# Attention and two mixtures on one core: the first group's product with w_out stands one group later, with three smaller edits

## Chip, cores and metric

The kernel runs on one core of a Trainium2 chip. The metric is the device time of one execution in microseconds; three runs of the kernel before had a median of 963.05 us (961.12 to 963.38).

## What is computed

Three layers stand behind one another. The reference, cut to what matters:

```python
scores = where(sink | window, q @ k.T / sqrt(D), -1e9)   # 4 x 8 heads, 768 positions, D = 64
x  = softmax(scores) @ v                                  # 4 sinks, window of 128; x: 3072 x 512
h  = maximum(maximum(x @ w1, x @ w2), x @ w3)             # 512 -> 768
x2 = h @ w_out                                            # 768 -> 512
# routing: the (token, expert) pairs of x2 @ w_gate in falling order, at most 384 tokens per expert
out[mask_e] = relu(x2[mask_e] @ u1[e]) @ u2[e]            # 8 experts, 512 -> 1024 -> 512
```

## The kernel before, in words

**Tokens** come in 8 groups of 384. For each group, four pairs of heads go through attention (`Attn`), then the first mixture (`Moe1.group`, L295 on), then the product with w_out (`Moe1.x2`, L322 on). Products are kept near single precision by splitting each operand into a high and a low part (an ACT copy and a DVE subtraction, L28 and L29) and summing three matmuls.

**Attention** of one pair: scores on PE (L141 to L144), masked into a tile T by DVE (L147 to L155), softmax on ACT (L160 to L163), a product on POOL (L166), transposes on PE (L25 into `pt` and `pp`), DVE masks (L182), the product with v on PE (L189 to L202), and the result in `x0` to `x3`, one tile for each of the four pairs. `group` splits these four into X[0] to X[3] before its matmuls; each X has one buffer, so the split waits for the last matmul of the group before.

**The first mixture** of a group has 6 x 3 sums of 12 matmuls of 384 columns (L308), each into one of the two `mm` banks, taken out by ACT (L310) or DVE (L311); the last of three is split into H[f] in the tile `HL` (L316, L317).

**The product with w_out**: `x2` makes 3 x 2 sums of 18 matmuls of 260 columns (L333) from H, into `mm`. Group 0 can't do this at its place, since w_out isn't loaded yet: it writes its six maxima to HBM (`sp`), and `reload` (L345 on) reads them back through the two-deep tile `hm` (L350, on SP's queue), splits them on ACT (L352) and DVE (L353) into the parts of `HL` that the x2 ahead of it has read, and x2 follows. This stands where `g==back`.

**Order.** The loop over groups emits the attention of group g+1 inside group g (`between`, at sums 0, 1, 3 and 4), for group 2 ahead of group 1 (`order1`, with the six loads of w_out in the middle; `emit` raises its priority by `off=60` instructions). One planner orders each engine's instructions from the order in the code, these priorities and its own costs; tiles of a pool are handed out in the order of the code, so group 3 can't have an `mm` bank before the x2 that stands ahead of it.

**Logits.** Groups 5 to 7 multiply H with w_out @ w_gate (`logits`, L370 on): 12 matmuls (L375) into a bank, an ACT copy (L377), and in `rest`, which the next group calls after its sum (1,0), three transposes into a bank and one DVE reduction (L382).

**Routing and experts.** `Route.phase` finds an expert's threshold in six levels; each level is a count on PE (24 matmuls, L435), a short chain on DVE that ends in a comparison (L430), and the next count. `Moe2.expert` has 8 first products (12 matmuls, L637) and 8 second ones (9 matmuls of 512 columns, L630), 168 matmuls in all. The counts for an expert two further on run between them: `behind` ties the i-th count behind the matmul whose place in the expert's list stands in a tuple.

**The last expert** ends with the second products of f=6 and f=7: rows 0 and 1 for f=6, then for f=7, then row 2 for both. Of each row's sum ACT copies one half (L650) and DVE the other (L651), and POOL scatters the row (L652).

```python
for ts in ((0,1),(2,)): second(F-2,ts); second(F-1,ts)
nc.scalar.activation(o if s.n<7 else o[:,0:256],acc[t] if s.n<7 else acc[t][:,0:256],AF.Copy)
if s.n==7: nc.vector.tensor_copy(o[:,256:512],acc[t][:,256:512])
```

Of the kernel before, what the change touches and what calls it, by code (L numbers as in the profile page):

```python
# [221 lines left out]

class Moe1:
    def __init__(s, tc, words,wgate, consts, wpool, main, conv, mm, pt, pss, ident):
        s.tc=tc; s.nc=tc.nc; s.mm=mm; s.pss=pss; s.main=main; s.conv=conv; s.ident=ident; s.consts=consts
        s.src=words; s.wgate=wgate
        s.W=[[wpool.tile([128,4,768],FR,name=f"w{i}{x}") for x in "hl"] for i in range(3)]
        s.WO=None; s.at=None; s.stage=None; s.HL=None; s.nx=0; s.second=None; s.n=0; s.loads=[]
        s.WG=main.tile([128,6,16],FR,name="wgt")
# [139 lines left out]
            nc.scalar.dma_start(x2d[(t0+t)*128:(t0+t+1)*128,:],o)  # L369
    def logits(s,H,t0,LG):  # L370
        nc=s.nc; main=s.main
        ps=s.mm.tile([128,512],FT,name="mm")
        for f in range(6):
            for b in range(2):
                nc.tensor.matmul(ps[0:16,:384],s.WG[:,f,:],H[f][b],start=(f==0 and b==0),stop=(f==5 and b==1))  # L375
        lt=main.tile([128,520],FT,name="xo",bufs=1)[0:16,:384]
        nc.scalar.activation(lt,ps[0:16,:384],AF.Copy)  # L377
        def rest():
            p=s.mm.tile([128,512],FT,name="mm")
            for t in range(3):  # L380
                flip(nc,p[:,t*16:(t+1)*16],lt[:,t*128:(t+1)*128],s.ident[0:16,0:16])
            nc.vector.tensor_reduce(LG[:,t0:t0+3,:],p[:,0:48].rearrange("p (t b e) -> p t e b",t=3,b=2),axis=AX.X,op=OP.add)  # L382
        return rest
# [183 lines left out]
class Moe2:  # L567
# [53 lines left out]
    def expert(s,X,ev,idx,mid=None):  # L621

        nc=s.nc; F=8; s.n+=1; s.mms=[]
        acc=[s.acc.tile([128,512],FT,name=f"acc{t}") for t in range(3)]
        H=[None]*F; W=[None]*F
        def second(f,ts=range(3)):
            for t in ts:
                n=0
                for a,b in ((0,0),(0,1),(1,0)):
                    s.mms.append(nc.tensor.matmul(acc[t],H[f][a][:,t*128:(t+1)*128],W[f][1][b],start=(f==0 and n==0),stop=(f==F-1 and n==2))); n+=1  # L630
        for f in range(F):
            if f==5 and mid is not None: mid()
            W[f]=s.weights(ev,f)
            ps=s.mm.tile([128,512],FT,name="mm"); n=0
            for k in range(4):
                for a,b in ((0,0),(0,1),(1,0)):
                    s.mms.append(nc.tensor.matmul(ps[:,:384],W[f][0][a][:,k,:],X[k][b],start=(n==0),stop=(n==11))); n+=1  # L637
            h,l=(s.part(x,4+f%2) for x in "hl")
            with s.tc.high_priority():
                nc.scalar.activation(h,ps[:,:384],AF.Relu)  # L640
                nc.vector.scalar_tensor_tensor(l,ps[:,:384],0.0,f32(h),op0=OP.max,op1=OP.subtract)  # L641
            H[f]=(h,l)
            if f and (s.n<7 or f<F-1): second(f-1)
        if s.n<7: second(F-1)
        else:
            for ts in ((0,1),(2,)): second(F-2,ts); second(F-1,ts)
        for t in range(3):
            o=s.act.tile([128,512],FT,name="og",bufs=3)
            with s.tc.high_priority():
                nc.scalar.activation(o if s.n<7 else o[:,0:256],acc[t] if s.n<7 else acc[t][:,0:256],AF.Copy)  # L650
                if s.n==7: nc.vector.tensor_copy(o[:,256:512],acc[t][:,256:512])  # L651
            st=nc.gpsimd.indirect_dma_start(out=s.out,out_offset=bass.IndirectOffsetOnAxis(ap=idx[:,t:t+1],axis=0),in_=o,in_offset=None)  # L652
            for q in s.scat: s.tc.declare_no_dep(st.ins,q.ins,reason="other rows")
            s.scat.append(st)

def attention_mixtures(tc,q,k,v,vs,words,wg,u1,u2,out,off=60,spread=(0,1,3,4),native=8,order='a0 a0 a0 a0 w a1 w a1 w a1 w a1 w w a2',order1='a2 o o o o o o a2 a2',back=1,at=(1,0),s1=300,s2=400,nring=6):
    nc=tc.nc
    PS=bass.MemoryType.PSUM
    with ExitStack() as ctx:
# [4 lines left out]
        mm=P("mm",2,space=PS); pst=P("pst",1,space=PS)  # L664
# [71 lines left out]
        def behind(gs,mms,places):  # L736

            for ins,at in zip(gs,places):
                for i in ins:
                    tc.add_manual_dep(i.ins,mms[at].ins.name,mybir.DependencyInfo(mybir.DependencyClass.NoSync,mybir.DependencyReason.DATA),reason="order on TensorE")  # L740
# [22 lines left out]
        for n in range(8):  # L763
            r.groups=[]
            if n<6:
                with tc.high_priority(offset=s2): S.append(step(n+2)); fet(n+2)
            gs,r.groups=r.groups,[]
            E.expert(*G[n],mid=(lambda: trn(n+1)) if n<7 else None)
            if n<6: behind(gs,E.mms,(40,71,92,105,118,131,144,156,165,167) if n==0 else (20,75,85,95,106,117,131,145,156,160) if n==1 else (20,69,79,91,104,117,131,145,156,160) if n<5 else (4,16))


_INS = ['q', 'k', 'v', 'vs', 'words', 'wg', 'u1', 'u2']
# [50 lines left out]
```

## Time and profile before

| | |
|---|---|
| median of three runs | 963.05 us (961.12 to 963.38) |
| the profiled execution's own time | 959.1 us |
| its span, first to last instruction | 957.3 us |
| TensorE (PE) busy | 926.2 us, 97% |
| VectorE (DVE), ScalarE (ACT), GpSimd (POOL) busy | 702.3, 486.5, 256.3 us |
| mean granted TensorE clock | 0.993 |

Matmuls are pipelined: one of 384 columns has a record of about 0.34 us, while the next one starts about 0.17 us behind it. So a stop of PE shows as idle time only as far as it is longer than the tail of the last record; the starts tell it whole. Where the text speaks of a stop, it is the time from start to start less the usual one. The 1.8 us between span and time lie outside the instructions.

### The profile page before, as it was taken

Reading aid. Unit: us, or ns where it says so; the run is one execution under the profiler, and the core shown is the slowest. Engines: PE = TensorE matmul, PEld = TensorE weight load, DVE = VectorE, ACT = ScalarE, POOL = GpSimd, SP = SyncE. Lnnn points to the kernel's source line nnn. Section 1 sums busy time; section 2 is a strip of 40 time slices with the busy share of each in tenths; the row PEclk is TensorE's granted clock in tenths of the full one; section 3 lists DMA queues with packets and bytes.
Section 4 is the critical chain, followed back from the end, with each engine's and each line's share of the span. In section 5 each row is a group of like instructions: output and inputs, shape, how many; then the busy total and the mean of one; then the engine's idle time right before and its main releaser. Section 6 shows DMA issues by size and latency. Waiting matters only on the chain.

```text
span 957.3 us, 18496 instructions
## 1 busy us (share of the span) xinstructions
PE 926.2 (97%) x6552; PEld 849.3 (89%) x6552; DVE 702.3 (73%) x1870; ACT 486.5 (51%) x1329; POOL 256.3 (27%) x271
## 2 busy tenths in 40 slices
PE   6999999989999999999999999999999999999996
PEld 4688899979999999999999998888888888888895
DVE  7876786787887886678885435888999989873321
ACT  5466664776767685576773211433334434344431
POOL 5676536131321221221221000011203122053331
PEclk8999999999999999999999999999999999999999
DMA  8454322332122221122210002634445353564420
GB/s 234 141 196 154 113 79 79 98 116 74 54 69 70 59 82 42 53 80 92 66 57 1 1 1 89 222 115 133 132 135 177 115 163 116 160 188 163 130 70 33
DMA packets 54443, 99.35 MB, mean 104 GB/s; under 512 B 7792, under 2 KB 24688, under 8 KB 54352
## 3 DMA queue, kind: packets, MB, share of 16 engines
q1 hardware_dynamic: 44464, 75.90, 26.3%
q0 software_dynamic: 3840, 12.45, 3.8%
q10 hardware_dynamic: 6048, 9.83, 2.7%
q8 instruction: 51, 0.84, 0.4%
q14 instruction: 40, 0.33, 0.1%
HBM read 82.17 MB, written 16.12 MB: 103 GB/s over the span
## 4 chain that ended last, share of the span: by engine, by line
PE 80%; DVE 7%; issue 5%; ACT 4%; DMA 2%; POOL 1%; SPq 0%; POOLq 0%; DVEq 0%; ACTq 0%
PE mm L308 28%; PE mm L637 12%; PE acc L630 12%; PE mm L333 8%; PE po L201 3%; PE rc L435 3%; PE po L191 2%; PE ps L141 2%; PE pt L25 2%; PE pp L25 2%; PE ps L143 1%; PE ps L144 1%; ACT T_w L162 1%; PE acc L365 1%; PE po L202 1%
## 5 line engine op out<-in xcount | busy, mean ns | idle before, releaser
L630 PE MATMUL acc<-wbh,HL 128*128 128x512 f32 x384 | 132.2, 400 | 0.0
L311 DVE TENSOR_TENSOR hm<-mm,hm 128x384 f32<-128x384 f32 x96 | 53.1, 553 | 50.2 <-PE mm L308 49.1
L333 PE MATMUL mm<-woh,HL 128*128 128x260 f32 (+1 forms) x432 | 87.0, 291 | 2.5 <-ACT xo L335 1.2
L630 PEld LDWEIGHTS acc<-wbh,HL 128*128 128x128 f32 x384 | 71.4, 188 | 12.9 <-ACT HL L640 0.4
L581 ACT ACTIVATE wah<-sa 128x512 fp32r<-128x512 f32 x64 | 40.4, 631 | 83.3 <-PE mm L637 65.6
L581 ACT ACTIVATE wbh<-sb 128x512 fp32r<-128x512 f32 x64 | 40.4, 631 | 72.9 <-PE acc L630 67.3
L630 PE MATMUL acc<-wbl,HL 128*128 128x512 f32 x192 | 76.9, 401 | 0.0
L652 POOL DMA_INDIRECT out_dram<-og,idx x24 | 29.3, 1222 | 170.6 <-ACT og L650 141.0
L333 PEld LDWEIGHTS mm<-woh,HL 128*128 128x128 f32 x432 | 69.3, 191 | 4.5 <-ACT xo L335 1.9
L637 PE MATMUL mm<-HL,wah 128*128 128x384 f32 x256 | 67.6, 341 | 0.0
L308 PE MATMUL mm<-xh,w1h 128*128 128x384 f32 x192 | 66.0, 344 | 0.8 <-ACT hm L310 0.5
L308 PE MATMUL mm<-xh,w0h 128*128 128x384 f32 x192 | 66.6, 347 | 0.0
L308 PE MATMUL mm<-xh,w2h 128*128 128x384 f32 x192 | 66.2, 345 | 0.2 <-ACT hm L310 0.2
L308 PE MATMUL mm<-xl,w0h 128*128 128x384 f32 x192 | 65.4, 341 | 0.0
L641 DVE SCALAR_TENSOR_TENSOR HL<-mm,HL 128x384 fp32r<-128x384 f32 x64 | 35.4, 554 | 40.6 <-ACT HL L640 38.5
L308 PE MATMUL mm<-xh,w1l 128*128 128x384 f32 x192 | 65.2, 340 | 0.0
L308 PE MATMUL mm<-xh,w0l 128*128 128x384 f32 x192 | 64.9, 338 | 0.0
L308 PE MATMUL mm<-xl,w2h 128*128 128x384 f32 x192 | 64.8, 338 | 0.0
L308 PE MATMUL mm<-xl,w1h 128*128 128x384 f32 x192 | 64.8, 337 | 0.0
L308 PE MATMUL mm<-xh,w2l 128*128 128x384 f32 x192 | 64.6, 337 | 0.0
L582 DVE TENSOR_TENSOR wbl<-sb,wbh 128x512 fp32r<-128x512 f32 x64 | 44.0, 688 | 25.0 <-ACT wbh L581 23.6
L333 PE MATMUL mm<-wol,HL 128*128 128x260 f32 (+1 forms) x216 | 61.9, 288 | 0.0
(335 smaller groups left out, 2781.9 us busy)
## 6 DMA issues: line engine op xcount, KB each, us to landing
sa<-in_u_dram SPq DMA_DIRECT2D x64, 256.0 KB
sb<-in_u_dram SPq DMA_DIRECT2D x64, 256.0 KB
HL<-in_words_dram SPq DMA_DIRECT2D x18, 512.0 KB
qn<-in_q_dram SPq DMA_DIRECT2D x88, 96.0 KB
x2d<-xo ACTq DMA_DIRECT2D x15, 256.0 KB
kn<-in_k_dram SPq DMA_DIRECT2D x12, 264.0 KB
st<-in_words_dram SPq DMA_DIRECT2D x6, 512.0 KB
vn<-in_v_dram SPq DMA_DIRECT2D x12, 256.0 KB
```

The lines of the kernel that those rows point to most:

```text
L25: nc.tensor.transpose(out,x,f32(ident))
L201: nc.tensor.matmul(po[:,q:q+n],u['VS'][:,blk,128*h:128*h+128],part[:,c:c+n],start=(part is H and j==0),stop=False,skip_group_check=True)
L308: nc.tensor.matmul(ps[:,:384],s.W[i][a][:,p,f*128:(f+1)*128],X[p][b],start=(n==0),stop=(n==11)); n+=1
L311: else: nc.vector.tensor_tensor(m,ps[:,:384],m,op=OP.max)
L333: mms.append(nc.tensor.matmul(ps[:,:n],H[f][a][:,t*128:(t+1)*128],s.WO[b][:,f,u,c],start=(k==0),stop=(k==17))); k+=1
L435: s.put([s.nc.tensor.matmul(pc[0:s.M,0:k],s.OHR[:,c],TH[:,c,0:k],start=(c==0),stop=(c==23)) for c in range(*r)])
L581: nc.scalar.activation(h,src,AF.Copy)
L582: (nc.gpsimd if s.n>=6 and nm=="wa" else nc.vector).tensor_tensor(l,src,f32(h),op=OP.subtract)
L630: s.mms.append(nc.tensor.matmul(acc[t],H[f][a][:,t*128:(t+1)*128],W[f][1][b],start=(f==0 and n==0),stop=(f==F-1 and n==2))); n+=1
L637: s.mms.append(nc.tensor.matmul(ps[:,:384],W[f][0][a][:,k,:],X[k][b],start=(n==0),stop=(n==11))); n+=1
L641: nc.vector.scalar_tensor_tensor(l,ps[:,:384],0.0,f32(h),op0=OP.max,op1=OP.subtract)
L652: st=nc.gpsimd.indirect_dma_start(out=s.out,out_offset=bass.IndirectOffsetOnAxis(ap=idx[:,t:t+1],axis=0),in_=o,in_offset=None)
```

## The change

`back` goes from 1 to 2: group 0's reload and x2 stand behind group 2's x2 and ahead of group 3. The logits of t0=18 (group 6) and their `rest` take the bank of the pool `pst` (tile `pt`), which attention used for the sinks' transposes, in place of two `mm` banks. In the last expert each row's sum is finished (f=6, then f=7) before the next row's, and ACT copies all 512 columns. For expert 1 the second to sixth count are tied behind matmuls 74, 86, 97, 108, 119 (75, 85, 95, 106, 117 before), for experts 2 to 4 the third and fourth behind 81 and 92 (79 and 91 before).

```diff
--- before.py
+++ after.py
@@ -222,7 +222,7 @@
 
 class Moe1:
     def __init__(s, tc, words,wgate, consts, wpool, main, conv, mm, pt, pss, ident):
-        s.tc=tc; s.nc=tc.nc; s.mm=mm; s.pss=pss; s.main=main; s.conv=conv; s.ident=ident; s.consts=consts
+        s.tc=tc; s.nc=tc.nc; s.mm=mm; s.pss=pss; s.pt=pt; s.main=main; s.conv=conv; s.ident=ident; s.consts=consts
         s.src=words; s.wgate=wgate
         s.W=[[wpool.tile([128,4,768],FR,name=f"w{i}{x}") for x in "hl"] for i in range(3)]
         s.WO=None; s.at=None; s.stage=None; s.HL=None; s.nx=0; s.second=None; s.n=0; s.loads=[]
@@ -369,14 +369,15 @@
             nc.scalar.dma_start(x2d[(t0+t)*128:(t0+t+1)*128,:],o)
     def logits(s,H,t0,LG):
         nc=s.nc; main=s.main
-        ps=s.mm.tile([128,512],FT,name="mm")
+        bank=(lambda: s.pt.tile([128,512],FT,name="pt")) if t0==18 else (lambda: s.mm.tile([128,512],FT,name="mm"))
+        ps=bank()
         for f in range(6):
             for b in range(2):
                 nc.tensor.matmul(ps[0:16,:384],s.WG[:,f,:],H[f][b],start=(f==0 and b==0),stop=(f==5 and b==1))
         lt=main.tile([128,520],FT,name="xo",bufs=1)[0:16,:384]
         nc.scalar.activation(lt,ps[0:16,:384],AF.Copy)
         def rest():
-            p=s.mm.tile([128,512],FT,name="mm")
+            p=bank()
             for t in range(3):
                 flip(nc,p[:,t*16:(t+1)*16],lt[:,t*128:(t+1)*128],s.ident[0:16,0:16])
             nc.vector.tensor_reduce(LG[:,t0:t0+3,:],p[:,0:48].rearrange("p (t b e) -> p t e b",t=3,b=2),axis=AX.X,op=OP.add)
@@ -643,17 +644,16 @@
             if f and (s.n<7 or f<F-1): second(f-1)
         if s.n<7: second(F-1)
         else:
-            for ts in ((0,1),(2,)): second(F-2,ts); second(F-1,ts)
+            for t in range(3): second(F-2,(t,)); second(F-1,(t,))
         for t in range(3):
             o=s.act.tile([128,512],FT,name="og",bufs=3)
             with s.tc.high_priority():
-                nc.scalar.activation(o if s.n<7 else o[:,0:256],acc[t] if s.n<7 else acc[t][:,0:256],AF.Copy)
-                if s.n==7: nc.vector.tensor_copy(o[:,256:512],acc[t][:,256:512])
+                nc.scalar.activation(o,acc[t],AF.Copy)
             st=nc.gpsimd.indirect_dma_start(out=s.out,out_offset=bass.IndirectOffsetOnAxis(ap=idx[:,t:t+1],axis=0),in_=o,in_offset=None)
             for q in s.scat: s.tc.declare_no_dep(st.ins,q.ins,reason="other rows")
             s.scat.append(st)
 
-def attention_mixtures(tc,q,k,v,vs,words,wg,u1,u2,out,off=60,spread=(0,1,3,4),native=8,order='a0 a0 a0 a0 w a1 w a1 w a1 w a1 w w a2',order1='a2 o o o o o o a2 a2',back=1,at=(1,0),s1=300,s2=400,nring=6):
+def attention_mixtures(tc,q,k,v,vs,words,wg,u1,u2,out,off=60,spread=(0,1,3,4),native=8,order='a0 a0 a0 a0 w a1 w a1 w a1 w a1 w w a2',order1='a2 o o o o o o a2 a2',back=2,at=(1,0),s1=300,s2=400,nring=6):
     nc=tc.nc
     PS=bass.MemoryType.PSUM
     with ExitStack() as ctx:
@@ -766,7 +766,7 @@
                 with tc.high_priority(offset=s2): S.append(step(n+2)); fet(n+2)
             gs,r.groups=r.groups,[]
             E.expert(*G[n],mid=(lambda: trn(n+1)) if n<7 else None)
-            if n<6: behind(gs,E.mms,(40,71,92,105,118,131,144,156,165,167) if n==0 else (20,75,85,95,106,117,131,145,156,160) if n==1 else (20,69,79,91,104,117,131,145,156,160) if n<5 else (4,16))
+            if n<6: behind(gs,E.mms,(40,71,92,105,118,131,144,156,165,167) if n==0 else (20,74,86,97,108,119,131,145,156,160) if n==1 else (20,69,81,92,104,117,131,145,156,160) if n<5 else (4,16))
 
 
 _INS = ['q', 'k', 'v', 'vs', 'words', 'wg', 'u1', 'u2']
```

## Rows read from the trace of the kernel before

**Rows 1.** The page's head and its section 1: span, and PE's busy time.

```profile
span 957.3 us, 18496 instructions
...
PE 926.2 (97%) x6552; PEld 849.3 (89%) x6552; DVE 702.3 (73%) x1870; ACT 486.5 (51%) x1329; POOL 256.3 (27%) x271
```

**Rows 2.** Windows: length, busy us (instructions) of PE, PEld, DVE, ACT, POOL; clock; DMA.

```profile
187.00:207.00 20.00, 16.99 (x106) 13.18 (x105) 17.89 (x36) 16.17 (x55) 8.48 (x8) 0.98 0.44 138
207.00:219.00 12.00, 12.00 (x92) 12.00 (x92) 9.00 (x17) 9.36 (x35) 1.51 (x1) 0.89 0.32 96
219.00:274.00 55.00, 55.00 (x366) 54.69 (x365) 45.40 (x94) 38.68 (x117) 15.49 (x20) 1.00 0.21 59
274.00:292.00 18.00, 18.00 (x153) 17.97 (x152) 13.79 (x28) 13.03 (x42) 2.96 (x4) 1.00 0.27 84
```

**Rows 3.** The same windows for the matmuls of line L333 (x2) alone.

```profile
187.00:207.00 20.00, 6.45 (x36) 4.88 (x36) 0.98 0.44 138
207.00:219.00 12.00, 10.06 (x72) 9.78 (x72) 0.89 0.32 96
```

**Rows 4.** The chain that ended last: start, us, what (two x2 sums without a stop).

```profile
214.47 4.39 PE mm L333 x36
```

**Rows 5.** PE's timeline, 194 to 210 us: start, us, instruction [idle before, releaser].

```profile
196.78 0.90 PE L333 MATMUL mm<-woh,HL 128*128 128x260 f32 x2 [0.80 <-DVE HL L353]
...
205.97 0.39 PE L143 MATMUL ps<-kh_w,qs 128*128 128x260 f32 x1 [1.43 <-DVE T_x L153]
```

**Rows 6.** ACT's timeline, 196 to 205 us: a split of the reload.

```profile
196.72 0.52 ACT L352 ACTIVATE HL<-hm 128x384 fp32r<-128x384 f32 x1 [0.80 <-DMA hm<-sp]
```

**Rows 7.** DVE's timeline, 202 to 208 us: the last split of the reload, and X[3]'s.

```profile
202.40 0.56 DVE L353 TENSOR_TENSOR HL<-hm,HL 128x384 fp32r<-128x384 f32 x1
...
206.90 0.55 DVE L29 TENSOR_TENSOR xl<-x,xh 128x384 fp32r<-128x384 f32 x1
```

**Rows 8.** PE's timeline around the logits of t0=18 and their rest.

```profile
540.62 0.34 PE L375 MATMUL mm<-HL,wgt 128*16 128x384 f32 x1
541.43 0.44 PE L308 MATMUL mm<-xh,w1h 128*128 128x384 f32 x1 [0.46 <-ACT hm L310]
...
547.98 0.35 PE L25 MATMUL mm<-ident,xo 16*128 16x16 f32 x3
548.64 0.45 PE L308 MATMUL mm<-xh,w1h 128*128 128x384 f32 x1 [0.30 <-DVE LG L382]
```

**Rows 9.** PE's timeline in expert 3: the third and fourth count.

```profile
780.42 0.51 PE L637 MATMUL mm<-HL,wah 128*128 128x384 f32 x2
781.27 0.77 PE L435 MATMUL rc<-th,ohr 128*128 128x32 bf16 x24 [0.34 <-DVE th L430]
...
784.36 0.52 PE L435 MATMUL rc<-th,ohr 128*128 128x32 bf16 x14
```

**Rows 10.** DVE's timeline in expert 3: the comparison ahead of the fourth count.

```profile
783.13 0.56 DVE L430 TENSOR_TENSOR th<-z,thr 128x768 bf16<-128x768 bf16 x1
```

**Rows 11.** PE's waits, 680 to 860 us: total, times, longest (the only row).

```profile
PE rc L435 <- DVE th L430: 1.5, 4, 0.6
```

**Rows 12.** ACT's timeline at the end: the last two of three half copies.

```profile
948.59 0.38 ACT L650 ACTIVATE og<-acc 128x256 f32<-128x256 f32 x1 [0.32 <-PE acc L630]
949.99 0.38 ACT L650 ACTIVATE og<-acc 128x256 f32<-128x256 f32 x1 [1.02 <-PE acc L630]
```

**Rows 13.** DVE's timeline at the end: the last low part of H, the last half copy.

```profile
946.32 0.56 DVE L641 SCALAR_TENSOR_TENSOR HL<-mm,HL 128x384 fp32r<-128x384 f32 x1 [3.62 <-ACT HL L640]
...
950.40 0.42 DVE L651 COPY og<-acc 128x256 f32<-128x256 f32 x1 [0.97 <-ACT og L650]
```

**Rows 14.** POOL's timeline at the end: first and last of three scatters.

```profile
949.01 0.99 POOL L652 DMA_INDIRECT out_dram<-og,idx  x1 [26.49 <-DVE og L651]
...
951.57 0.96 POOL L652 DMA_INDIRECT out_dram<-og,idx  x1 [0.31 <-issue]
```

**Rows 15.** Groups by line and shape: the whole copies of the other experts (busy us, mean ns).

```profile
L650 ACT ACTIVATE og<-acc 128x512 f32<-128x512 f32 x21 | 12.6, 598 | 2.6 <-PE acc L630 1.3
```

## The prediction

> **What bounds the kernel now.** I read the page's head first: PE is busy for 926.2 of 957.3 us [rows 1], so only stops of PE can be won back, and they have to be found one by one. I read PE's timeline from start to start and found four places that the change touches. The windows come next. In 187 to 219 us, between group 1's x2 and group 2's first matmul, PE is idle for 3.0 us and its granted clock is 0.98 and then 0.89 of full, while DVE is busy for 17.89 of 20 us; in the 73 us behind it PE never stops and the clock is 1.00 [rows 2]. Group 0's x2 stands in that poor stretch [rows 3].
>
> How much is lost there: 36 matmuls of x2 need 4.39 us when nothing stops them [rows 4], so the 108 of one x2 need 13.2. The other records, attention, are PE's busy time less that of x2: 16.99 - 6.45 = 10.5 and 12.00 - 10.06 = 1.9 us [rows 2, 3]. 32.0 - 13.2 - 12.5 leaves **6.3 us lost**: 3.0 idle, 1.3 + 0.4 by the clock (0.11 of 12 us, 0.02 of 20), the rest hidden under the tails of records. What ended the stops is told by PE's timeline: a split of the reload, and DVE being late with attention [rows 5].
>
> **1. The x2 of group 0 moves (`back`).** Its 108 matmuls, 6 + 3 copies on ACT, 12 splits (6 on ACT, 6 on DVE), 6 loads on SP's queue and 3 stores on ACT's all stay; they leave the stretch at 187 us and come between group 2's x2 and group 3. PE's 13.2 us are neither won nor lost. What changes is who covers whom.
>
> At the old place they cover a late X[3]. Group 2 needs it for the last 3 of each sum's 12 matmuls, and its split ends in 207.45 [rows 7], 20 us behind the end of group 1's x2. With x2 gone PE has until then only attention and, in the two `mm` banks, the 9 matmuls of each sum that go without X[3]: 18, which start 0.17 us apart (a record of two is 0.51 long, of one 0.34 [rows 8, 9]), or 3.1 us. But X[3] should come sooner: the reload's six DVE splits of 0.56 and six ACT splits of 0.52 us [rows 6, 7] leave the queues that its chain runs through, 6.4 us together. Bounds: not sooner at all (207.45), and by all of it (201.0). I take 5 us, 202.4, since most of them stand in front of one of the chain's steps. PE then has 9 us of attention (10.5 less what stands behind 202.4) and 3.1 us of group 2 in 15.4 us: 3.3 lost. By the bounds it is 1.9, or 6.9 (20.45 - 10.5 - 3.1) and another 1.3 by the clock.
>
> At the new place the reload is a chain again: each split waits for the x2 ahead of it to have read that part of `HL`, loads 3 to 6 for `hm`, two at a time, and SP's queue issues them among the loads of attention; ACT waited 0.80 us for one of them [rows 6]. While it runs, no matmul of group 3 can fill in (the `mm` banks are handed out in order), only attention of group 4. No trace shows this; the nearest rows are the old place's. Its stops that the reload itself ended come to 1.4 us (0.80 idle, 0.16 under the tail, and the pair of 196.78 that takes 0.90 where 0.40 is usual) [rows 5]; bounds: 0.3, as group 2's x2 loses now next to no time [rows 2], and 6.3, if all the loss goes along. I take 1.4. DVE is free enough: 45.40 of 55 us in group 2 [rows 2]. **Sum of this part: -6.3 + 3.3 + 1.4 = -1.6 us**, by the bounds from -4.1 to +8.2.
>
> **2. The logits' bank.** Now the logits of t0=18 hold one of the two `mm` banks until the last H is split, so group 7's second sum waits for the first one's copy: from 540.62 to 541.43 are 0.81 us where 0.17 is usual, 0.64 lost. In `rest` the next sum waits for DVE's reduction: 547.98 to 548.64 are 0.66 where three transposes need 0.19 (0.35 less a tail of 0.16), 0.47 lost [rows 8]. In the bank of attention's transposes, idle by then (group 7's attention lies behind), neither wait exists; ACT's copy and DVE's reduction stay and nobody waits for them. **-1.1 us**; bounds 0 (another wait falls due there) and -1.3.
>
> **3. The counts' places.** In expert 3 the third count would follow the matmul pair of 780.42 in 780.77 and starts in 781.27, when DVE's comparison ends: 0.50 lost [rows 9]. There are four such stops in experts 1 to 4 [rows 11]. Two more matmuls ahead of it (0.35 us) leave 0.15 in experts 2 to 4: -1.05. The fourth count then follows one matmul sooner (0.23), and its comparison has ended in 783.69, 0.67 before the count [rows 9, 10]: no new wait. In expert 1 the second count moves up by one matmul and the third back by one: about 0.2 of its stop. **-1.2 us**; bounds 0 and -2.1 (1.5 idle [rows 11] and four tails of 0.16).
>
> **4. The last expert.** The sums now end with 6, 12 and 18 matmuls instead of 9, 12 and 18. Row 1's copy starts in 948.59, row 2's in 949.99, so a matmul is 0.233 us, and row 0 would be ready in 947.19 instead of 947.89 [rows 12]. Only three matmuls of f=6 instead of six now cover H[7]: its low part is ready in 946.88 [rows 13], and row 0's sixth matmul wants it some 0.4 us ahead of 947.19, so a stop of 0.15 which all three rows inherit. The copy: now ACT's half and DVE's follow each other (949.99 + 0.38, then 950.40 + 0.42): 0.83 us; the whole one takes 0.60 [rows 12, 13, 15]. POOL issues three scatters 1.28 us apart from 949.01, so the third, in 951.57, waits for POOL and not for its row [rows 14]. Then: row 0's scatter 947.34 + 0.60 + 0.29 = 948.23 (0.29 as before, 947.89 + 0.83 to 949.01), the third no sooner than 950.79 by POOL, and by its row 949.99 + 0.15 + 0.60 + 0.29 = 951.03. **-0.5 us**; bounds -0.8 and +0.15. The Trainium skill speaks against this edit (Perfetto Trace Analysis, Optimizing Scalar/DVE Operations: where ACT or DVE only hold others up, breaking up instructions may let the work end sooner). By that rule halves would run side by side and end 0.42 after the sum, and the whole copy would cost 0.18 us; the rows show one behind the other, so I go by them.
>
> **The sum**: -1.6 - 1.1 - 1.2 - 0.5 = -4.4 us, from 959.1 us of the profiled execution to 954.7. That execution lies 4.0 us below the median of the runs; I carry the difference over: 963.05 - 4.4 = **958.6 us**.
>
> **Rivals.** A measurement of this kernel can tell about 0.3%, 2.9 us, from no change.
>
> *Slower: PE stands still for X[3].* DVE's queue is full there (17.89 of 20 us [rows 2]); if attention of group 3 moves into the time that the reload leaves, X[3] comes no sooner than 207.45. Then 6.9 us are lost at the head of group 2 and 1.3 by the clock, and if the whole old loss comes back behind group 2's x2 too, the part costs 8.2 instead of giving 1.6: 963.05 + 8.2 - 2.8 = 968.5 us. The point from which the kernel is slower at all is X[3] in about 206.8 (12.1 of work and 7.7 of loss behind 187). For it: one wait in one place would be long, and behind the stops of rows 5 the clock of 207 to 219 is 0.89. The Trainium skill (TensorE: Matmul & The Clock Gate, HAM oscillation) says that a waiting PE is throttled and starts the next work at half clock; the trace agrees with its 0.89, and a single long wait would be worse by it than many short ones. Against it: the chain of X[3] runs through ACT and DVE next to the very splits that go. Chance 0.15.
>
> *No change: the loss goes along.* Late attention and a reload in sequence lose as much at the one place as at the other (part 1 is 0), and the planner, which orders anew, gives half of parts 2 and 3 back elsewhere: -1.6, 961.4 us. That includes the case that counts or logits end up where they were. Chance 0.25.
>
> *All is won.* X[3] comes in 201, and group 2's x2 with the reload behind it has attention enough: part 1 at -4.1 and part 3 at -2.1, -7.8: 955.2 us. Chance 0.12.
>
> **The numbers.** My forecast has 0.48. Faster by over 0.3% (below 960.2): 0.48 + 0.12 = 0.60; within 0.25; slower (above 965.9) 0.15. The range from 953.0 to 966.0 takes in the two milder rivals and half of the way to the slower one, and leaves about 0.06 below it and 0.13 above. The forecast's own range is 955 to 961.
>
> **What the profile of the changed kernel would show.** Right: no L333 between some 187 and group 2's first L308, which starts before 206 us; clock near 1.00 in that stretch; L352 and L353 near 265 to 290; no stop in front of group 7's second sum; third counts with stops near 0.15 us; the third scatter 0.5 us sooner before the end. Wrong: a wait of PE L308 for an L29 of over 5 us, a clock below 0.9 near 200, or waits of L333 for L353 and for attention's DVE work of over 4 us behind group 2.

## The result, and the profile after

The changed kernel takes **975.66 us** (median of 5 runs, 975.08 to 976.56) where the kernel before took 961.42 beside it: a ratio of 1.0144, 95% interval 1.0127 to 1.0162. It is 14 us slower. The forecast was 958.6, from the 963.05 of the first three runs, with a range of 953.0 to 966.0; it was wrong in sign and size.

The page's head of the changed kernel, against [rows 1]:

```profile
span 974.4 us, 18527 instructions
...
PE 933.8 (96%) x6552; PEld 852.4 (87%) x6552; DVE 709.8 (73%) x1867; ACT 488.1 (50%) x1329; POOL 259.2 (27%) x271
```

PE issues the same 6552 matmuls. Its busy time is 7.6 us more (tails of records and a slower clock), and the other 9.5 of 17.1 us are idle. To see where, cut the span at the groups' first and last matmuls of L308. The windows of the kernel before (us, busy us of PE, PEld, DVE, ACT, POOL, clock, DMA): group 1's x2 and group 0's; group 2; group 2's x2; group 3; group 3's x2.

```profile
167.10:219.40 52.30, 49.29 (x352) 44.77 (x350) 40.54 (x87) 39.67 (x143) 11.50 (x10) 0.97 0.35 106
219.40:273.40 54.00, 54.00 (x358) 53.71 (x357) 44.63 (x92) 37.68 (x115) 15.49 (x20) 1.00 0.21 57
273.40:292.00 18.60, 18.60 (x157) 18.57 (x156) 14.39 (x29) 13.62 (x43) 2.96 (x4) 1.00 0.30 89
292.00:342.00 50.00, 50.00 (x321) 49.72 (x320) 42.37 (x76) 33.85 (x104) 10.27 (x12) 1.00 0.22 62
342.00:361.80 19.80, 18.77 (x157) 18.48 (x155) 17.06 (x33) 15.08 (x49) 5.42 (x6) 1.00 0.31 94
```

The same five stages of the changed kernel; group 0's x2 is now in the third:

```profile
168.00:187.60 19.60, 19.60 (x152) 18.90 (x151) 13.41 (x35) 13.60 (x52) 1.51 (x1) 1.00 0.22 67
187.60:263.10 75.50, 70.34 (x436) 63.66 (x435) 69.12 (x127) 55.26 (x184) 21.52 (x24) 1.00 0.26 75
263.10:319.40 56.30, 49.16 (x363) 46.72 (x362) 52.14 (x97) 46.61 (x150) 16.41 (x18) 0.94 0.36 110
319.40:364.70 45.30, 45.30 (x284) 45.10 (x283) 32.73 (x65) 26.72 (x88) 7.48 (x8) 1.00 0.16 49
364.70:382.40 17.70, 16.07 (x134) 15.86 (x133) 7.09 (x12) 7.50 (x19) 2.58 (x3) 1.00 0.14 47
```

Idle time alone hides stops under tails, so for each stage I added up, over PE's timeline, how much each matmul started later than is usual behind the one before it ("lost", good to about 1 us a row):

| stage | length before | after | lost before | after |
|---|---|---|---|---|
| to group 2's first L308 | 52.2 | 19.6 | 7.6 | 0.3 |
| group 2 | 54.0 | 75.5 | 1.8 | 12.1 |
| to group 3's first L308 | 18.7 | 56.4 | 0.4 | 14.0 |
| group 3 | 50.0 | 45.3 | 0.9 | 0.7 |
| to group 4's first L308 | 19.7 | 17.7 | 1.8 | 2.4 |
| group 4 to the end of group 7 | 216.9 | 211.6 | 10.4 | 7.9 |
| sum | 411.5 | 426.1 | 22.9 | 37.4 |

The whole difference of the runs (14 us) stands in the last row: +14.5. It comes in two places. **Old place** (first two rows): 9.4 lost becomes 12.4, though the product and its reload are gone. Group 2 ends 11.2 us sooner against the start of group 1's x2 (95.1 instead of 106.3 us), and 13.2 us of work have left. DVE is busy there for 13.41 + 69.12 of 95.1 us, and of the 5.2 us that PE stands idle in group 2 it waits 4.1 for DVE, never longer than 1.0 at a time (the two longest of PE's waits there: in total, times, longest):

```profile
PE ps L143 <- DVE T_x L153: 1.6, 2, 1.0
PE mm L308 <- DVE hm L311: 1.4, 2, 0.8
```

X[3] comes little sooner than before, [rows 7]:

```profile
206.17 0.55 DVE L29 TENSOR_TENSOR xl<-x,xh 128x384 fp32r<-128x384 f32 x1
```

That is 18.6 us behind the end of group 1's x2, where it was 19.9. **New place** (third row): 0.4 lost becomes 14.0, at a granted clock of 0.94. Some 9 us of it stand in 284 to 306 us, where the clock is 0.84, a mean of its two levels (2.4 and 1.2 GHz):

```profile
284.00:306.00 22.00, 17.35 (x105) 15.67 (x105) 21.43 (x39) 18.37 (x61) 5.85 (x7) 0.84 0.44 131
```

Behind a stop of 1.84 us, the one of 291.66 below, matmuls of 260 columns start 0.22 us apart where 0.12 is usual [rows 4], which is the lower level:

```profile
293.80 0.42 PE L333 MATMUL mm<-woh,HL 128*128 128x260 f32 x1
294.02 0.42 PE L333 MATMUL mm<-wol,HL 128*128 128x260 f32 x1
```

As an estimate, the clock took at most 0.16 of 22 us, 3.5 us, of the 14.0; the rest is stops. PE's timeline there, 264 to 303 us, the matmuls before which PE stood idle longest (the bracket: for how long, and for whom):

```profile
267.52 0.39 PE L333 MATMUL mm<-woh,HL 128*128 128x260 f32 x1 [1.17 <-DVE hm L311]
...
273.78 0.39 PE L143 MATMUL ps<-kh_x,qs 128*128 128x260 f32 x1 [1.32 <-DVE T_w L153]
...
288.03 0.51 PE L333 MATMUL mm<-woh,HL 128*128 128x260 f32 x2 [0.46 <-DVE HL L353]
...
291.66 0.56 PE L201 MATMUL po<-H,vsp 128*128 128x256 f32 x3 [1.84 <-DVE x L204]
...
300.35 0.55 PE L25 MATMUL pt<-ident,T_w 128*128 128x128 f32 x3 [0.85 <-POOL T_w L166]
...
302.19 0.56 PE L333 MATMUL mm<-woh,HL 128*128 128x260 f32 x2 [0.96 <-DVE HL L353]
```

Over the stretch PE stands idle for 1.9 us until a split of the reload is done (L352, L353), for 3.9 until attention is (L153, L204, L166), and for 1.2 until group 2's own maximum is (L311). The reload's loads on SP's queue are issued in pairs, since `hm` is two deep:

```profile
261.36 8.52 SPq L350 DMA_DIRECT2D hm<-sp  x2
...
288.00 1.62 SPq L350 DMA_DIRECT2D hm<-sp  x2
...
294.26 0.80 SPq L350 DMA_DIRECT2D hm<-sp  x2
```

and the second and third pair's first copies on ACT start 3.3 and 3.5 us behind them. ACT was busy with attention up to either copy, so a part of this is its own queue; where it did stand and wait for a load, in the kernel before, the copy came 2.4 us behind the issue (194.34 to 196.72 [rows 6]):

```profile
291.27 0.51 ACT L352 ACTIVATE HL<-hm 128x384 fp32r<-128x384 f32 x1
...
297.78 0.53 ACT L352 ACTIVATE HL<-hm 128x384 fp32r<-128x384 f32 x1
```

Last, DVE's timeline shows where the lead of attention ends. In the changed kernel the last half of group 4's attention and the first of group 5's (L204):

```profile
325.98 0.56 DVE L204 TENSOR_TENSOR x<-po,x 64x384 f32<-64x384 f32 x1
...
365.87 0.55 DVE L204 TENSOR_TENSOR x<-po,x 64x384 f32<-64x384 f32 x1
```

and the same two in the kernel before:

```profile
329.89 0.56 DVE L204 TENSOR_TENSOR x<-po,x 64x384 f32<-64x384 f32 x1
...
345.49 0.54 DVE L204 TENSOR_TENSOR x<-po,x 64x384 f32<-64x384 f32 x1
```

Group 4's attention ends at about the same time in both. Then the next write has to wait until `x0` has been split into X[0], which has one buffer, and that is when group 3's matmuls end: 364.7 instead of 342.0. The gap is 39.9 us instead of 15.6. At group 4's first matmul the changed kernel is 20 us behind (382.4 against 361.8). No run gave X a second buffer, so that this is what limits the lead rests on these rows.

**The small edits.** The logits of t0=18 go through the transposes' bank; of two stops of 0.64 and 0.47 [rows 8] there is one left, of 0.28 (559.41 - 558.95 less the usual 0.18):

```profile
558.95 0.33 PE L376 MATMUL pt<-HL,wgt 128*16 128x384 f32 x1
559.41 0.44 PE L308 MATMUL mm<-xh,w2h 128*128 128x384 f32 x1
```

The counts still stop PE four times (PE's waits, 690 to 880 us, against [rows 11]); by the starts, the third counts of experts 2 to 4 now stop for 0.15 us, as reckoned, but the second ones for 0.46:

```profile
PE rc L436 <- DVE th L431: 1.4, 4, 0.5
```

At the end, the last low part of H on DVE, and first and last of the whole copies on ACT and of the scatters on POOL, against [rows 12 to 14]:

```profile
963.93 0.56 DVE L642 SCALAR_TENSOR_TENSOR HL<-mm,HL 128x384 fp32r<-128x384 f32 x1 [3.65 <-ACT HL L641]
```

```profile
965.19 0.60 ACT L651 ACTIVATE og<-acc 128x512 f32<-128x512 f32 x1 [1.29 <-PE acc L631]
...
967.75 0.60 ACT L651 ACTIVATE og<-acc 128x512 f32<-128x512 f32 x1 [0.80 <-PE acc L631]
```

```profile
966.07 0.99 POOL L652 DMA_INDIRECT out_dram<-og,idx  x1 [25.93 <-ACT og L651]
...
968.63 0.96 POOL L652 DMA_INDIRECT out_dram<-og,idx  x1 [0.30 <-ACT og L651]
```

From the low part to the third scatter it is 4.70 us, where it was 951.57 - 946.32 = 5.25: 0.55 won. Every profiled execution with this edit has 4.69 or 4.70, and both without it have 5.25.

### The profile page after: what moved, and what is told of

Its sections match the earlier page's. It is cut to its first block, busy times and chain, and to the rows that moved or that the text cites. A ratio compares the mean times of both kernels' runs of the same rounds, so it can differ in the third digit from the quotient of the medians.

```text
span 974.4 us, 18527 instructions
## 1 busy us (share of the span) xinstructions
PE 933.8 (96%) x6552; PEld 852.4 (87%) x6552; DVE 709.8 (73%) x1867; ACT 488.1 (50%) x1329; POOL 259.2 (27%) x271
## 4 chain that ended last, share of the span: by engine, by line
PE 80%; DVE 9%; issue 5%; ACT 3%; DMA 2%; POOL 0%; SPq 0%; POOLq 0%; DVEq 0%; ACTq 0%
PE mm L308 27%; PE mm L638 12%; PE acc L631 12%; PE mm L333 8%; PE po L201 3%; PE rc L436 3%; PE po L191 2%; PE ps L141 2%; PE pt L25 2%; PE pp L25 2%; PE ps L143 1%; PE ps L144 1%; DVE m L159 1%; PE acc L365 1%; DVE L L197 1%
## 5 line engine op out<-in xcount | busy, mean ns | idle before, releaser
L311 DVE TENSOR_TENSOR hm<-mm,hm 128x384 f32<-128x384 f32 x96 | 53.2, 554 | 60.1 <-PE mm L308 56.1
L333 PE MATMUL mm<-woh,HL 128*128 128x260 f32 (+1 forms) x432 | 85.5, 289 | 3.1 <-DVE HL L353 1.7
L333 PEld LDWEIGHTS mm<-woh,HL 128*128 128x128 f32 x432 | 69.3, 191 | 5.1 <-DVE HL L353 2.4
L308 PE MATMUL mm<-xh,w0h 128*128 128x384 f32 x192 | 66.8, 348 | 1.3 <-ACT xh L28 0.7
L308 PE MATMUL mm<-xh,w2h 128*128 128x384 f32 x192 | 66.6, 347 | 0.8 <-ACT hm L310 0.7
L308 PE MATMUL mm<-xh,w1h 128*128 128x384 f32 x192 | 66.3, 345 | 0.8 <-DVE hm L311 0.8
L308 PE MATMUL mm<-xl,w0h 128*128 128x384 f32 x192 | 65.6, 341 | 0.0
L308 PE MATMUL mm<-xh,w1l 128*128 128x384 f32 x192 | 65.3, 340 | 0.0
L308 PE MATMUL mm<-xl,w2h 128*128 128x384 f32 x192 | 65.0, 339 | 0.0
L308 PE MATMUL mm<-xh,w0l 128*128 128x384 f32 x192 | 64.9, 338 | 0.0
L308 PE MATMUL mm<-xl,w1h 128*128 128x384 f32 x192 | 64.8, 337 | 0.0
L308 PE MATMUL mm<-xh,w2l 128*128 128x384 f32 x192 | 64.8, 337 | 0.0
L166 POOL TENSOR_TENSOR T_w<-T_w,l 128x792 f32<-128x792 f32 x21 | 32.1, 1529 | 114.1 <-DVE l L165 114.1
```

Of the source, the lines that this page charges most:

```text
L166: s.ev['s',u['n']]=nc.gpsimd.tensor_tensor(T,T,l[:,:,None].to_broadcast([128,6,132]),op=OP.mult)
L308: nc.tensor.matmul(ps[:,:384],s.W[i][a][:,p,f*128:(f+1)*128],X[p][b],start=(n==0),stop=(n==11)); n+=1
L311: else: nc.vector.tensor_tensor(m,ps[:,:384],m,op=OP.max)
L333: mms.append(nc.tensor.matmul(ps[:,:n],H[f][a][:,t*128:(t+1)*128],s.WO[b][:,f,u,c],start=(k==0),stop=(k==17))); k+=1
```

## The experiments

All ratios are to the kernel before, run beside each on the same chip; the intervals are of 95%. "Lost" is told as in the table above, from one profiled execution of each.

### Is it the move, or one of the small edits?

The changed kernel with the product at its old place:

```diff
-...,back=2,at=(1,0),...
+...,back=1,at=(1,0),...
```

> The changed kernel with group 0's x2 put back behind group 1's (back=1); the logits' bank, the counts' places and the last expert stay changed. If the move of x2 is the cause of the 14 us (both theories below), this stands at or a little under the kernel before: 959 to 961 us, by what the changed kernel's trace shows of the three small edits (0.55 at the end, 0.4 to 0.8 at the logits, nothing at the counts, whose stops only went from one count to the one ahead of it). If one of the small edits is the cause (theory S), it stands near 970 us or above.

And the kernel before with the move alone:

```diff
-...,back=1,at=(1,0),...
+...,back=2,at=(1,0),...
```

> The kernel before with back=2 alone. If the move is the cause: 976 to 978 us, what the changed kernel takes and the 1 to 1.5 us that the small edits gave. Theory S: 961 us.

Measured: 958.05 us, ratio 0.9987 (0.9973 to 1.0000), and 975.81, ratio 1.0166 (1.0133 to 1.0199). In the first the stages lose what they lost before (7.5, 1.8 and 0.4 in the first three), in the second what they lose after (11.8 in group 2, 13.9 behind it). **The move alone makes the kernel slower**, and the small edits have no part in it.

### What does the reload cost at either place?

The product of group 0 reads the H that is there (group 2's, or group 1's at the old place), so the 6 loads and 12 splits of the reload are left out and 384 rows of group 0 get another group's values:

```diff
-                    M.x2(M.reload(sp),0,LG,x2d)
+                    M.x2(H,0,LG,x2d)
```

At the new place:

> The changed kernel, in which x2 of group 0 multiplies the H of group 2 again: the six loads and twelve splits of the reload are left out (the 384 rows of group 0 get group 2's values), its 108 matmuls stay. Theory R (the reload's chain of loads and splits, with no matmul of group 3 to fill in, makes the 13.8 us that PE loses between 264 and 319 us): about 10 us come back, 964 to 967 us. Theory D (DVE is late with attention from 187 us on, since x2 no longer stands there as work for PE that needs no DVE; PE waits for DVE wherever it stands): only the reload's own DVE time comes back, 3.4 us of splits and perhaps some half clock: 970 to 973 us.

At the old one (with `back=1`):

> back=1 with the small edits, and x2 of group 0 takes group 1's H again: the reload's six loads and twelve splits are left out (the 384 rows of group 0 get group 1's values). It measures what the reload costs at the old place. If it costs there what it costs at the new one (12 us): 946 to 949 us. If the old place hides it but for the 1.4 us of stops that the prediction counted there: 956 to 957 us.

| ratio | product behind group 1 | behind group 2 |
|---|---|---|
| with the reload | 0.9987 (0.9973 to 1.0000) | 1.0144 (1.0127 to 1.0162) |
| without it | 0.9967 (0.9955 to 0.9980) | 1.0054 (1.0039 to 1.0070) |

Down the columns: the reload costs 0.0020, some 2 us, at the old place and 0.0090, some 9 us, at the new one. Along the rows: the move costs 0.0087, some 8 us, even when nothing has to be reloaded, and 15 with the reload. So **about half of the loss is the product's own place, and about half the reload at that place** (each difference is good to some 2 us). Without the reload the stretch behind group 2 loses 3.8 us instead of 14.0 (windows of the kernel without it, group 2 and the stretch behind it):

```profile
188.10:263.50 75.40, 70.25 (x436) 63.57 (x434) 69.06 (x127) 55.10 (x184) 21.54 (x24) 1.00 0.25 73
263.50:301.60 38.10, 35.58 (x294) 34.96 (x293) 28.53 (x55) 25.88 (x84) 9.08 (x10) 1.00 0.25 82
```

### Is PE's time at the old place free?

The changed kernel with group 1's product done twice, which puts 108 matmuls (13.2 us) of nothing where group 0's product stood:

```diff
-                elif g: M.x2(H,3*g,LG,x2d)
+                elif g:
+                    M.x2(H,3*g,LG,x2d)
+                    if g==1: M.x2(H,3*g,LG,x2d)
```

> The changed kernel with group 1's x2 done twice in a row: 108 matmuls, 13 us of PE work that asks for almost nothing of DVE, stand again where group 0's x2 stood before, and nothing else changes. Theory D: PE had no work there that DVE could feed, so the added 13 us cost 0 to 4 us: 976 to 980 us. Theory R, or PE simply being the bound there: they cost 10 to 13 us, 986 to 989 us.

Measured: 976.54 us, ratio 1.0180 (1.0145 to 1.0216), 0.0036 above the changed kernel: 3.5 us for 13.2 us of work (good to some 4 us). The windows from group 1's end to group 2's first matmul, and of group 2:

```profile
168.10:209.50 41.40, 41.40 (x310) 38.02 (x310) 22.48 (x50) 22.91 (x80) 7.01 (x8) 1.00 0.22 69
209.50:262.90 53.40, 53.40 (x353) 53.28 (x352) 45.15 (x91) 39.70 (x128) 12.44 (x14) 1.00 0.23 70
```

Group 2 ends in 262.9, and without the filler in 263.1. PE has no idle time at all: most of the filler stands where PE stopped before. Not all of it, though. The changed kernel has 152 + 436 matmuls in these two windows, so the filler should make 696, and there are 663: 33 matmuls of attention, 3.9 us of PE's work, now follow behind group 2's end, about what the kernel is longer by. So some 9 of the 13 us were free. Nor is the end near 263 one limit: with the filler PE is busy throughout and DVE for 67.6 of 94.8 us, without it DVE for 82.5 of 95.1 and PE waits for it. The kernel without the reload at the old place shows the same as the filler:

```profile
168.20:209.60 41.40, 41.40 (x310) 38.01 (x309) 22.50 (x50) 22.84 (x80) 7.02 (x8) 1.00 0.22 69
209.60:263.00 53.40, 53.40 (x352) 53.28 (x351) 45.18 (x91) 39.68 (x128) 12.39 (x14) 1.00 0.22 65
```

So the 11.2 us by which the changed kernel's group 2 ends sooner are owed to the reload's leaving; the product's leaving gave no sooner end, only those 33 matmuls of attention ahead of it. And even of that lead little lasts: the kernel without the reload is 11.5 us ahead at group 2's end of the one with it at the same place, and 0.0020, 2 us, in the end. Nearly half of the lead is work put off (46 of attention's matmuls, 5.2 us, stand behind group 2's end instead of ahead of it), and its later stages lose more (2.5 behind group 2 instead of 0.4, 2.6 in group 3 instead of 0.9, 3.1 behind group 4 instead of 1.5), waiting for attention.

### What of the reload costs at the new place?

Loads straight into the low part of `HL`, with the subtraction in place, so that no two-deep `hm` limits them; at the new place and the old one:

```diff
-            m=s.main.tile([128,384],FT,name="hm",bufs=2)
-            nc.sync.dma_start(m,spill[f])
             h,l=s.part("h",f),s.part("l",f)
-            nc.scalar.activation(h,m,AF.Copy)
-            nc.vector.tensor_tensor(l,m,f32(h),op=OP.subtract)
+            nc.sync.dma_start(f32(l),spill[f])
+            nc.scalar.activation(h,f32(l),AF.Copy)
+            nc.vector.tensor_tensor(l,f32(l),f32(h),op=OP.subtract)
```

> The changed kernel (x2 of group 0 behind group 2's) with another staging of the reload: each maximum is loaded straight into the low part's place in HL and split there in place, so all six loads can go out as soon as group 2's x2 has read HL, instead of two at a time through the two buffers of hm; the twelve splits stay. Theory R1 (the two-deep ring: three rounds of load and split, 284.6 to 304.2 us in the changed kernel's trace, of which the second and third load take 3 us each): two rounds of load fall away but the first load can't be fetched ahead any more: net 3 to 6 us come back, 970 to 973 us, and up to 10 if the splits close ranks. Theory R2 (the splits stand behind attention in DVE's queue; DVE is busy for 21.4 of 22 us there): little comes back, 973 to 976 us.

> The same staging with x2 of group 0 back at its old place behind group 1's (back=1; the small edits stay). The filler run showed that 13 us of PE work without a reload cost nothing at the old place, while moving x2 with its reload away from there brought group 2's end 11 us nearer; so the reload costs about 11 us at the old place too. R1: 950 to 955 us. R2: 956 to 959 us, as back=1 with the old staging (958.05).

Measured: 973.33 us, ratio 1.0117 (1.0095 to 1.0140), and 960.56, ratio 1.0005 (0.9989 to 1.0021). The stretch behind group 2 loses 8.6 instead of 14.0, but the stage behind group 3 gives back 1.6 and groups 5 to 7 as much; 2.6 us (0.0027, no more than the two intervals leave open) are left of 5.4. At the old place it gives nothing.

The splits first in their queues:

```diff
-            nc.scalar.activation(h,m,AF.Copy)
-            nc.vector.tensor_tensor(l,m,f32(h),op=OP.subtract)
+            with s.tc.high_priority():
+                nc.scalar.activation(h,m,AF.Copy)
+                nc.vector.tensor_tensor(l,m,f32(h),op=OP.subtract)
```

> The changed kernel (back=2), the reload's twelve splits marked with high priority, so that the planner puts them ahead of attention's instructions on ACT and DVE; loads and staging as they were. R2 (the splits' place in DVE's queue): 6 to 9 us come back, 966 to 970 us. R1 (the ring of two): 0 to 3 us, 973 to 976 us.

Measured: 974.97 us, ratio 1.0152 (1.0128 to 1.0177). Inconclusive: the planner's order of instructions in this stretch stayed the same, so the splits weren't moved.

The six subtractions on GpSimd, at the new place and the old one:

```diff
-            nc.vector.tensor_tensor(l,m,f32(h),op=OP.subtract)
+            nc.gpsimd.tensor_tensor(l,m,f32(h),op=OP.subtract)
```

> The changed kernel (back=2) with the reload's six subtractions on POOL instead of DVE; ring of two, loads and ACT's half as they were. In the changed kernel's trace the six stand 1.8 to 2.6 us behind their ACT halves because DVE is full of attention. R2 (the splits' place in DVE's queue makes the loss behind group 2's x2): the loss there falls from 14.0 to 7 us or less, 967 to 970 us. R1 (the ring of two and its loads): 973 to 976 us. POOL's subtraction may itself take longer than DVE's 0.56 us; the run shows it.

> The same with x2 of group 0 at its old place (back=1). Leaving the reload out altogether gave 2 us over back=1 with it, although group 2 then ended 11 us sooner: the rest was given back in the groups behind. So at most 2 us are to be had: 956 to 958 us where the kernel before has 959 to 961. R1: no change, 958 to 960.

Measured: 975.24 us, ratio 1.0144 (1.0125 to 1.0164), and 963.95, ratio 1.0021 (1.0008 to 1.0034). This does take them out of DVE's queue (a subtraction takes 1.0 to 1.3 us on GpSimd), and the stretch still loses 15.1. So it isn't their place in DVE's queue; at the old place it is 3 us worse.

One load for all six splits, so that only the chain of splits is left (five loads left out, 384 rows of group 0 get other values):

```diff
-            m=s.main.tile([128,384],FT,name="hm",bufs=2)
-            nc.sync.dma_start(m,spill[f])
+            if f==0:
+                m=s.main.tile([128,384],FT,name="hm",bufs=2)
+                nc.sync.dma_start(m,spill[f])
```

> The changed kernel with one load for the reload: all six copies and subtractions read the first row block, so five of the six loads are left out (384 rows of group 0 get other values); the twelve splits stay. Theory L (the loads set the pace of the reload, some 3 us from issue to landing, two at a time): the stretch between group 2 and group 3 loses about 5 us instead of 14.0, and the time comes near that of the kernel without the reload, 964 to 967 us. Theory C (the chain of splits behind attention's work on DVE and ACT sets the pace): the stretch still loses 10 us or more and the time stays at 972 us or above.

Measured: 971.62 us, ratio 1.0128 (1.0105 to 1.0150). Both theories are half right. **The loads do set the pace of the stretch**: it loses 5.6 us instead of 14.0, as the first theory said. (The planner then also puts the six copies on ACT in one row, 285.41 to 287.49, so the run shows the loads together with the order that is made for them.) But the time hardly moves, as the second said, since the next stages lose more: 3.2 instead of 0.7 in group 3, 6.8 instead of 2.4 behind it. There PE waits 2.1 us for DVE, which is late with group 3's own H:

```profile
366.39 0.51 PE L333 MATMUL mm<-woh,HL 128*128 128x260 f32 x2 [2.10 <-DVE HL L317]
```

Attention of group 4 runs alongside; in the changed kernel it used the stops (16.7 us of PE's work of attention stand in the stretch, here 10.2) and now falls into group 3. Time won in this stretch is mostly not kept as long as attention has to be done as well.

### Is every later place as bad?

The product one group further on again:

```diff
-...,back=2,at=(1,0),...
+...,back=3,at=(1,0),...
```

> The changed kernel with the product one group further on again, behind group 3 (back=3). Theory L (the reload is a chain of its own wherever it stands): the stretch behind group 3 loses about 10 us more than the 2.4 of the changed kernel, the old place loses what it loses there, and the time is 972 us or above. Theory A (it costs that much only where attention is late at the same time, as behind group 2): behind group 3, where DVE has only 7.6 us of work in 17.7, the loss is under 6 us and the time 962 to 970 us.

Measured: 964.55 us, ratio 1.0057 (1.0037 to 1.0076). The stretch behind group 3, which now has the product and the reload, loses 6.0 us instead of 14.0 for the same two:

```profile
339.60:383.20 43.60, 41.51 (x328) 39.52 (x327) 35.87 (x69) 32.90 (x109) 11.66 (x14) 1.00 0.33 100
```

(6.0 stands just at the edge of what the second theory gave it; the time is where it put it.) The same 6 loads and 12 splits cost far less one group later, so **it is not the reload by itself but the place**. That the places differ by how late attention is fits DVE's share (busy for 35.87 of 43.6 us here, for 52.14 of 56.3 behind group 2), but no run tests it alone. It is still some 5 us slower than before.

### Does less work on DVE for attention help?

Group 3's four pairs (12 to 15), whose attention runs in group 2, are taken in the other form that the code has for attention (`native`, so far in pairs 0 to 7, 10 and 11), with longer matmuls and less work on DVE:

```diff
-4*g+p in (10,11)
+4*g+p in range(10,16)
```

> The changed kernel (back=2) with the four pairs of heads of group 3's attention on the other path that the kernel has (as the first eight pairs): no splits of K and Q and none of the masked product on ACT and DVE, some 4.4 us of DVE work less per pair, at about the same PE time (one score matmul of 0.22 us for two of 0.12). These pairs run beside group 2. Theory D (without x2 at its old place PE waits for DVE's attention work through group 2: 12.1 us lost there): the loss in group 2 falls to 4 to 8 us and group 3's attention ends sooner, so less of it is left for the stretch behind: 962 to 970 us. If DVE is not what PE waits for in group 2, the time stays at 973 to 976 us.

> The same path for the same four pairs with x2 of group 0 at its old place (back=1) and the small edits. D: PE's 7.5 us of loss between group 1 and group 2 fall by some 2 to 5 us, 953 to 957 us, unless the groups behind give it back as they did without the reload (then 957 to 959). Not D: 958 to 960 us.

Measured: 976.76 us, ratio 1.0174 (1.0154 to 1.0194), and at the old place 976.05, ratio 1.0150 (1.0132 to 1.0169). DVE's busy time in group 2 falls from 69.1 to 46.7 us, and PE's stops there from 12.1 to 5.0 lost: DVE is what most of them waited for. But behind group 1 PE's work of attention grows by 7 us in all (98.7 to 105.7), and group 2 ends no sooner (265.3). At the old place the other form costs 16 us, and only 6 of them are work (99.1 to 105.2): the stretch ahead of group 2 does lose 4 us less, but all stages together lose 10 more, above all behind group 2 (6.0 instead of 0.4) and behind group 3 (6.2 instead of 1.6). A miss as a cure, and why the later stages stop so much more at the old place stays open.

### What are the small edits worth?

The three edits at the old place once more, and without the counts' new places, twelve runs each:

```diff
-(20,74,86,97,108,119,131,145,156,160) if n==1 else (20,69,81,92,104,117,131,145,156,160)
+(20,75,85,95,106,117,131,145,156,160) if n==1 else (20,69,79,91,104,117,131,145,156,160)
```

> The three small edits (logits' bank, counts' places, last expert) at the old place (back=1), now in five rounds. If they give what their rows show in single traces (0.8 and 0.55 us, the counts nothing that lasts): 1 to 1.5 us, a ratio near 0.9986. If they give the 2.8 us of the prediction: 0.997. If the planner takes it back elsewhere: 1.000.

> The same without the counts' new places: only the logits' bank and the last expert. If the places are worth their 1.2 us, this one is 1.2 us (0.12%) above the one with all three; if what a count waits for hangs on the execution and not on its place, both take the same time within 0.1%, and the stops at the counts add up to anything between 0.4 and 2.6 us in either.

Measured: 957.31 us both, ratios 0.9990 (0.9974 to 1.0006) and 0.9989 (0.9973 to 1.0004). No worth of the counts' places shows, though each ratio is only good to 0.0016, 1.5 us. What a count waits for differs from one execution to another: the stops in front of the 24 counts add up to 2.3 us with the old places in the profile of before, and to 0.47 with the same places in the kernel with the move alone and in this last one; with the new places to 2.6 in the changed kernel, to 0.8 in the kernel with the splits marked, whose instructions stand in the same order, and to 0.39 in both executions with the three edits at the old place. The fastest version found is thus the changed kernel with the product back at its old place. It beats the changed kernel by 1.6%; that it beats the kernel before (by 0.1%) isn't shown.

## Why the prediction was wrong

**The bound.** That only stops of PE can be won back holds: the +14.5 of lost time are the whole result.

**The step that failed is the first of part 1**: that PE's 13.2 us "are neither won nor lost", with its pair -6.3 + 3.3. It reckoned what is won at the old place as the work that leaves plus 3.0 us of stops, because X[3] would come 5 us sooner. It came 1.3 us sooner against group 1's x2, near the lower bound ("not sooner at all"). And X[3] wasn't the only wait: DVE was busy for 69 of the next 75.5 us, and PE stopped for it again and again (4.1 of 5.2 us idle in group 2). Of the 13.2 us that left, the filler shows some 9 to have stood where PE would have stopped. The loss went from 9.4 to 12.4 (+3.0 where -3.0 was forecast): the product had been cover. The rival "PE stands still for X[3]" had this in part: X[3] came hardly sooner, and the full DVE queue that it named (17.89 of 20 us [rows 2]) was the sign to follow. Its one long wait and its fall of the clock did not come (1.0 us at most, clock 1.00). It had 0.15.

**The second step that failed is the +1.4 for the reload at the new place**, with a bound of 6.3. It measured 13.6. The reload is not much longer there: from its first copy to its last subtraction 19.6 us (284.62 to 304.21), where it was 16.0 (186.94 to 202.96); and PE has much the same work beside it, two products and 146 of attention's matmuls instead of 133. But the same stage lost 7.6 us at the old place and loses 14.0 at the new one, more of it waiting for attention than for the splits (3.9 and 1.9 us of idle time; 1.9 and 0.8 at the old place), at a granted clock of 0.94 instead of 0.97. "All the loss goes along" was no upper bound: the old place kept its loss, and the reload made a larger one at the new place. The runs show 10.2 of the 14.0 gone with the reload left out and 8.4 with five loads left out. Why attention is later there stays open. What a place loses can't be bounded by what another place loses.

"DVE is free enough: 45.40 of 55 us in group 2" read the row of before, in which group 2 was covered by the x2 ahead of it. And no part of the working asked whether a lead in attention can be kept. By the rows it can't: group 5's attention started writing only in 365.87, when X was free. Of the signs that the forecast named, the last wrong one came true: behind group 2 PE stood idle for 4.8 us for L353 and for attention's DVE work.

**Part 2** was right in kind: one stop of 0.28 is left where 0.64 + 0.47 stood, so 0.8 for 1.1. **Part 3** fell: the third counts stop for 0.15 as reckoned, but the counts ahead of them stop instead, and in other executions the sum is 0.4 to 0.8, with the old places and with the new. One trace was taken for the kernel. **Part 4** held: -0.55 for -0.5, with copies of 0.60 and the third scatter waiting for its row instead of POOL, as reckoned. The 0.55 is that of the copies and the new order of the sums together. That a whole copy (0.60) beats two halves (0.83), against the rule of the Trainium skill (Perfetto Trace Analysis, Optimizing Scalar/DVE Operations), followed from the rows.

**The slower rival** gave 968.5; the result is 7 us beyond it, nearly all by its second half: at the old place it had 1.9 us more lost and 3.0 came, at the new one 6.3 and 13.6 came. The range left out everything above 966 with 0.13.

## What to carry to other kernels

A stop of PE inside a stretch that another engine paces is hardly a loss: most of the work that stands there is free (some 9 of 13 us here), and taking it out wins little, while it must be paid where PE is the bound. Before moving work off such a place, ask what sets the end of the stretch without it, and whether a lead won there can be kept by the buffers behind it. A chain of loads through a two-deep ring is not the same cost at two places (2 and 9 us here): look at what else is late at each.

## What the runs showed of the hardware

**Counts.** With PE's, ACT's and DVE's instructions in the same order (the changed kernel, and that with the splits marked), the stops in front of the counts of experts 1 to 4 were 2.6 us in one execution and 0.8 in another, and from the first expert's first matmul to the end of the span it was 317.5 and 315.5 us. A stop of 0.5 us in one trace need not be a property of the kernel.

**DVE beside GpSimd.** A subtraction of the reload took 1.25 us on DVE instead of 0.56 while GpSimd ran an operation of its own on SBUF (the changed kernel's timelines of DVE and of POOL):

```profile
300.89 1.25 DVE L353 TENSOR_TENSOR HL<-hm,HL 128x384 fp32r<-128x384 f32 x1
```

```profile
300.25 1.46 POOL L120 TENSOR_TENSOR vsp<-vn,vsp 128x384 fp32r<-128x384 f32 x1
```

Of the six, two were stretched so (1.37 and 1.25 us), and both lay beside this line of POOL for over 0.8 us; none of the other four did for more than 0.2, and they took 0.56. The Trainium skill (GPSIMD Engine Reference, Specifications) says that GpSimd's access to SBUF is shared with VectorE where a DVE instruction has two inputs in SBUF; these subtractions have two, and the rows agree. So do two larger operations of 128x768 in this trace: L197, with both inputs in SBUF, took up to 2.29 us beside GpSimd and never more than 0.96 away from it, while L182, with one input in PSUM, never took more than 0.96 beside it either.
